# Products of six pairs made in the last attention steps, a ring of weight tiles split in two, and four sums placed ahead of the last modes

## The chip, the cores and the metric

The kernel runs on one core of one Trainium2 chip. The metric is the device time of one execution in microseconds (us). A run's profile gives a span that is about 1.8 us shorter than its device time.

A ratio is the mean time of one kernel's fast runs over the mean of the other's fast runs of the same rounds on the same chip. It is therefore not quite the ratio of the medians that are also quoted. Brackets give the 95% interval.

## The reference

```python
x = attention(q, k, v, s)                 # 8 batches, 576 rows, 8 heads of 64 -> 512 columns
X = np.fft.rfft(x, axis=1)[:, :64]        # 64 modes
Yr = Xr @ w_r - Xi @ w_i                  # per mode; w_r, w_i: 64 x 512 x 512 in float32
Yi = Xr @ w_i + Xi @ w_r
y = np.fft.irfft(Y, n=576, axis=1)
u = x + y
return u + np.maximum(u @ w_ch, 0.0)
```

The weights w_r and w_i are 134 MB in float32. They are read once and cast to bfloat16 on the way.

## The kernel before

Attention takes 32 steps: four groups of heads, each with eight batches. The modes need the four groups of columns g in turn. Each g has eight groups of modes, called modes group 0 to 7 below, and each modes group reads four weight tiles of 512 KB. So there are 128 weight tiles. The modes of the last g run after attention. Between them stands the work on w_ch: for each pair of row tiles x@w_ch is made and kept ("z"), and y@w_ch is added at the end.

The parts that the change touches are these. The ring of weight tiles and the plan of its loads:

```python
WB = 17
wpool = ctx.enter_context(tc.tile_pool(name="w_sb", bufs=WB))
...
    w = W0 + (WB + NE - W0) * (n + 1) // (B + 1) if n < B else on_chip[-1] + 4
    on_chip.append(min(w, WB + (NE if used[n] < NE else used[n])))
```

The last stage, one modes group after the other, with units of x work between them (a unit is: transpose the x of one pair, multiply by w_ch, keep the result):

```python
TAKE = (3, 3, 1, 2, 4, 3)                 # units of x work in modes groups 0 to 5
for c in range(NCK - 2):
    yb = modes(NG - 1, c)
    for x in range(TAKE[c] - 1):
        work()
    yt = y_transposed(yb)
    work()
    y_times_wch(c, yt)                    # v = y@w_ch of the group; ends with spread(), a transfer into yv
work()
...
c = NCK - 2                               # modes group 6
yb = modes(NG - 1, c)
x_transposed(0)
yt = y_transposed(yb)
x_transposed(1)
y_times_wch(c, yt)
for i in range(NPRE):
    x_times_wch(i, False)
start_u(0)
add_y(us[0], 0, 0, slice(0, GK))
yb = modes(NG - 1, NCK - 1)               # modes group 7, the last weights
...                                       # y and v of group 7, in halves
spread(NCK - 1, 1, vb)
for i in range(NPRE):
    add_y(z_of(i), i, 1, slice(0, GK))    # "the four sums": y@w_ch of pairs 0 and 1, modes groups 0 to 6
for i in range(NPRE):
    for cols in halves:
        add_last(z_of(i), i, vb, cols)    # group 7, straight from its tile
    relu(i, 2 - i)
```

`add_y` reads yv, so it waits for the spreads of the modes groups that it sums. After this the 18 pairs are finished one after the other and written out.

The softmax here doesn't subtract the row's maximum and nothing guards it: scores larger than these inputs give would overflow.

Of the kernel before, what the change touches and what calls it, by code (L numbers as in the profile page):

```python
# [9 lines left out]
FP32 = mybir.dt.float32  # L10
FP16 = mybir.dt.float16
BF16 = mybir.dt.bfloat16
ACTF = mybir.ActivationFunctionType
ALU = mybir.AluOpType
# [4 lines left out]
def kernel(  # L19
# [26 lines left out]
    MC = 8  # L46
    NCK = NM // MC
    WM = 4
    WB = 17
    LA = 3  # L50
    NF = NT - 1
    R = S // (P // 2)
# [47 lines left out]
    Ff_sb = gp.tile([P, NT, 3 * NM], FP16, name="Ff_sb")  # L100
    G_sb = gp.tile([P, SP], FP16, name="G_sb")
    wch_sb = gp.tile([P, DT, DM], FP16, name="wch_sb")
    wpool = ctx.enter_context(tc.tile_pool(name="w_sb", bufs=WB))
    spool = ctx.enter_context(tc.tile_pool(name="small_sb", bufs=2))
    auxpool = ctx.enter_context(tc.tile_pool(name="aux_psum", bufs=2, space=PSUM))

# [78 lines left out]
    NE = len(early)  # L185
    wt = {}

    def loads_w(upto):
        todo = []
        while len(wt) < min(upto, len(wq)):  # L190
            g, c, ri, par = key = wq[len(wt)]
            if len(wt) < NE:
                t = early[len(wt)]
            else:
                t = wpool.tile([P, WM, DM], BF16, name="w_sb", tag="w")
            src = (moe_w_r, moe_w_i)[ri]
            todo.append((
                t,
                src[c * MC + par : (c + 1) * MC : 2, g * P : (g + 1) * P, :].rearrange("m p e -> p m e"),
            ))  # L200
            wt[key] = t
        return todo
# [14 lines left out]
    W0 = 3  # L217
    on_chip = []
    for n in range(N):
        w = W0 + (WB + NE - W0) * (n + 1) // (B + 1) if n < B else on_chip[-1] + 4  # L220
        on_chip.append(min(w, WB + (NE if used[n] < NE else used[n])))


    nc.sync.dma_start(out=s_sb, in_=s.rearrange("b h t -> (b h) t"))
# [70 lines left out]
    def transposes(n, which):  # L295
        if n >= N:
            return
        src = loaded[n][which]
        dA, dB = ((qtA, qtB), (ktA, ktB))[which]
        g, b = divmod(n, B)  # L300
        ps = trpool.tile([P, R, RP], BF16, name="tr_ps", tag="tr")
        for r in range(R):
            for h in range(2):
                rows = slice(D * h, D * h + D)
                nc.tensor.transpose(ps[rows, r, :], src[rows, r, :], ident16[rows, rows])  # L305
        for dst, rows in ((dA, slice(0, D)), (dB, slice(D, P))):
            copy = (nc.vector.tensor_copy, nc.scalar.copy)[which == 1 and dst is dB]
            copy(  # L308
                out=dst[n % NQ][rows, :].rearrange("d (p r) -> d p r", r=R),
                in_=ps[rows].rearrange("d r p -> d p r"),  # L310
            )
# [18 lines left out]
    def scores(n, h):  # L330
        g, b = divmod(n, B)
        pidx = b * H + 2 * g + h
        qt = (qtA, qtB)[h][n % NQ]
        pt = p_sb[(2 * n + h) % NP_]
        keys = (ktA, ktB)[h][n % NQ][:, : NF * P].rearrange("c (w p r) -> c w r p", p=P, r=2)
        for r in range(2):
            ps = scpool.tile([P, 1024], FP32, name="sc_ps", tag="sc")

            for w in range(NWN):
                nc.tensor.matmul(  # L340
                    ps[:, bass.ds(w * S, W)], ident16, negm[:, bass.ts(r, W)],
                    start=True, stop=False, skip_group_check=True,
                )
            for w, i0, i1 in ((0, 0, 512), (0, 512, S), (1, W, S)):
                c0 = w * S + i0 - w * W
                nc.tensor.matmul(  # L346
                    ps[:, c0 : c0 + i1 - i0], keys[:, w, r, :], qt[:, i0:i1],
                    start=False, stop=True, skip_group_check=True,
                )
            if h == 1 and r == 0:  # L350
                scores4(n, ps[:, 2 * S - W : 2 * S - W + NL])
            for w in range(NWN):
                x = 2 * w + r
                nc.scalar.activation(  # L354
                    out=pt[:, poff[x] : poff[x] + S - w * W], in_=ps[:, w * S : (w + 1) * S - w * W],
                    func=ACTF.Exp, bias=cumt_sb[:, x, pidx : pidx + 1], scale=0.125,
                )
# [53 lines left out]
    def modes(g, c):  # L411

        ps = auxpool.tile([P, DM], FP32, name="yp", tag="aux")
        for x in range(4):
            ri, par = divmod(x, 2)
            cols = xs[g % 2].rearrange("p k r b m -> p (k r b) m")
            c0 = (48, 16)[ri] - 16 * par
            for cg in range(4):
                nc.tensor.matmul(  # L419
                    ps[32 * cg : 32 * cg + 32, :],  # L420
                    cols[:, c0 : c0 + 32, c * MC + 2 * cg + par],
                    wt[(g, c, ri, par)][:, cg, :],
                    start=(x == 0), stop=(x == 3),
                    tile_position=(0, 32 * cg), skip_group_check=True,
                )
        if g == 0:
            nc.vector.tensor_copy(out=y_acc[:, c, :], in_=ps)
        elif g < NG - 1:
            nc.vector.tensor_tensor(out=y_acc[:, c, :], in0=ps, in1=y_acc[:, c, :], op=ALU.add)
        else:  # L430
            yb = spool.tile([P, DM], FP16, name="y_sb", tag="y")
            for cols in halves if c == NCK - 1 else [slice(0, DM)]:
                nc.vector.tensor_tensor(
                    out=yb[:, cols], in0=ps[:, cols], in1=y_acc[:, c, cols], op=ALU.add
                )
            spread(c, 0, yb)
            return yb
# [5 lines left out]
        nc.sync.dma_start(out=yv[16 * c : 16 * c + 16, :, which, :], in_=rows)  # L443


    with tc.tile_pool(name="sc_psum", bufs=2, space=PSUM) as scpool, \
            tc.tile_pool(name="tr_psum", bufs=1, space=PSUM) as trpool, \
            tc.tile_pool(name="av_psum", bufs=1, space=PSUM) as avpool:
        cum_rows(0)
        transposes(0, 0)  # L450
        transposes(0, 1)
        load(loads_qkv(2))
        pad_p()
        for n in range(N):
            if n in (0, 2):
                nc.vector.memset(xs[n // 2].rearrange("p k r b m -> p (k r b m)").bitcast(FP32), 0.0)
            tails_due = loads_tails(n // B + 1)[n % B - 3 : n % B - 2] if 2 < n % B < 5 else []
            load(loads_qkv(n + LA) + tails_due, loads_w(on_chip[n]))
            cum_rows(n + 1)
            scores(n, 0)  # L460
            av(n - 1, 1)
            transposes(n + 1, 0)
            scores(n, 1)
            transposes(n + 1, 1)
            fft(n - 1)
            av(n, 0)
            for c in mode_steps.get(n, []):
                modes(c // NCK, c % NCK)
            if n == N // 2:
                nc.gpsimd.dma_start(out=wch_sb, in_=moe_w_ch.rearrange("(dt p) e -> p dt e", p=P))  # L470
        av(N - 1, 1)
        fft(N - 1)
    load(loads_w(len(wq)))
    at.close()




    pairs = [((b, T), (b, T + 1)) for b in range(B) for T in range(0, NF, 2)]
    for i, b in ((4, 0), (10, B // 2)):  # L480
        pairs.insert(i, ((b, NF), (b + 2, NF)))
    NPRE = 2
    kept = list(range(NPRE, len(pairs)))


    ways = dict(zip(kept, "esesessesesseses"))

    finpool = ctx.enter_context(tc.tile_pool(name="fin_sb", bufs=1))
    yv = finpool.tile([P, B, 2, DM], FP16, name="yv")
# [11 lines left out]
    places = [finpool.tile([P, 4 * DM], BF16, name=f"z1_{i}") for i in range(NLOC)]  # L501
    places.append(old[:, 4 * DM : 8 * DM])
    places += [y_acc[:, c : c + 2, :].rearrange("p c e -> p (c e)").bitcast(BF16) for c in (0, 2)]
    xts, z1s, zs = {}, {}, {}

    def parts(b, T):

# [24 lines left out]

    def keep(i):
        x_times_wch(i, True)
        j = kept.index(i)
        if j < len(places):
            t = places[j]
        else:
            t = wpool.tile([P, WM, DM], BF16, name="z1", tag="w").rearrange("p m e -> p (m e)")
        if ways[i] == "e":  # L540
            z1s[i] = t.bitcast(FP16).rearrange("p (y x e) -> p y x e", y=2, x=2)
            nc.scalar.copy(out=z1s[i][:, 0], in_=zs[i])
            nc.vector.tensor_tensor(
                out=z1s[i][:, 1], in0=zs[i], in1=z1s[i][:, 0], op=ALU.subtract
            )
        else:
            z1s[i] = t.bitcast(FP32).rearrange("p (x e) -> p x e", x=2)
            nc.scalar.copy(out=z1s[i], in_=zs[i])  # L548

    def y_transposed(yb):  # L550
        ps = auxpool.tile([P, DT, P], FP16, name="yt_ps", tag="aux")
# [29 lines left out]
            i = ahead.pop(0)  # L581
            keep(i)

    order_z = list(kept)
    TAKE = (3, 3, 1, 2, 4, 3)
    us, rs = {}, {}
    GK = P - 2 * MC

# [61 lines left out]
    def z_of(i):  # L650
        return [zs[i][:, x, :] for x in range(2)]

    for c in range(NCK - 2):
        yb = modes(NG - 1, c)
        for x in range(TAKE[c] - 1):
            work()
        yt = y_transposed(yb)
        work()
        y_times_wch(c, yt)
    work()  # L660
    assert not order_z and not ahead
# [9 lines left out]

    start_u(0)
    add_y(us[0], 0, 0, slice(0, GK))
    yb = modes(NG - 1, NCK - 1)

    yt = spool.tile([P, DT, P], FP16, name="yt_sb", tag="yt")
# [13 lines left out]
            )  # L690
        nc.vector.tensor_copy(out=vb[:, cols], in_=vp)
    spread(NCK - 1, 1, vb)
    for i in range(NPRE):
        add_y(z_of(i), i, 1, slice(0, GK))
    for i in range(NPRE):
        for cols in halves:
            add_last(z_of(i), i, vb, cols)
# [71 lines left out]
```

## Time and profile before

| | before |
|---|---|
| device time | 461.0 us (460.58 to 461.66, 3 runs) |
| profiled run | 462.23 us, span 460.4 us |
| PE busy | 342.2 us, 74% |
| DMA row of the slices | full to slice 36 of 40 |
| last weight tile lands (profiled run) | 421.56 us |
| work after that | 38.8 us; PE has one gap there (0.53 us), and its last matmul ends at 455.6 us |

The chain that ended last, in shares by engine (the chain line of the page), says how much rests on transfers:

```profile
DMA 70%; PE 21%; issue 3%; DVE 3%; POOL 2%; SPq 0%; DVEq 0%; POOLq 0%
```

### The profile page before, as it was taken

The page shows a single profiled execution, that of the slowest core. Times are in us where ns is not written, and L with a number is a line of the kernel's source. Part 1 is how long each engine was busy: PE and PEld are TensorE (multiplying, and loading weights), DVE is VectorE, ACT ScalarE, POOL GpSimd, SP SyncE. Part 2 cuts the span into 40 slices and gives each one's busy share as a digit, 9 for nine tenths or more (in the row PEclk, how much of TensorE's full clock was granted, in tenths as well). Part 3 has the DMA queues.
Part 4 walks back from the last instruction along what each step waited for, and adds up shares of the span by engine and source line. Part 5 has one row for each costly group of instructions (what it writes and reads, how often), then busy time and mean ns, then how long its engine had stood idle before and what let it go on. Part 6 is the DMA issues. An engine that isn't in the chain of part 4 may idle for free.

```text
span 460.4 us, 10238 instructions
## 1 busy us (share of the span) xinstructions
PE 342.2 (74%) x4153; PEld 217.0 (47%) x4185; DVE 233.2 (51%) x521; ACT 218.4 (47%) x376; POOL 183.0 (40%) x269
## 2 busy tenths in 40 slices
PE   1779888974667668876666757567959858988995
PEld 1456666653445446654444534344635424544432
DVE  6775666663334346644334443334445625562675
ACT  1585876563444427744244342444602303340895
POOL 6754555544445455434544434444422222100000
PEclk9997999998777879978778795777878979999999
DMA  9999999999999999999999999999999999994697
GB/s 173 200 203 204 201 202 203 203 204 204 204 202 203 203 201 203 204 204 203 203 202 205 205 204 204 204 204 204 204 210 210 212 215 213 211 212 89 229 309 296
DMA packets 110063, 95.16 MB, mean 207 GB/s; under 512 B 28544, under 2 KB 105216, under 8 KB 110016
## 3 DMA queue, kind: packets, MB, share of 16 engines
q0 software_dynamic: 98960, 81.81, 112.2%
q1 hardware_dynamic: 11056, 12.70, 9.1%
q8 instruction: 33, 0.54, 0.4%
q14 instruction: 14, 0.11, 0.1%
HBM read 164.66 MB, written 9.44 MB: 378 GB/s over the span
## 4 chain that ended last, share of the span: by engine, by line
DMA 70%; PE 21%; issue 3%; DVE 3%; POOL 2%; SPq 0%; DVEq 0%; POOLq 0%
DMA w_sb<-in_moe_w_i_dram 31%; DMA w_sb<-in_moe_w_r_dram 25%; DMA q<-in_q_dram 7%; PE sc_ps L346 3%; PE sc_ps L340 2%; DMA wch_sb<-in_moe_w_ch_dram 2%; DMA v<-in_v_dram 2%; PE av_ps L375 2%; PE z_ps L593 2%; PE u_ps L612 2%; PE u_ps L593 2%; PE tr_ps L305 2%; PE yp L419 1%; PE z_ps L712 1%; PE z_ps L528 1%
## 5 line engine op out<-in xcount | busy, mean ns | idle before, releaser
L354 ACT ACTIVATE p_sb<-sc_ps,cumt_sb 128x576 f16<-128x576 f32 (+1 forms) x256 | 142.2, 635 | 57.2 <-PE sc_ps L346 57.0
L208 POOL DMA_DIRECT2D w_sb<-in_moe_w_i_dram x60 | 45.1, 753 | 74.8 <-PE yp L419 19.6
L208 POOL DMA_DIRECT2D w_sb<-in_moe_w_r_dram x60 | 45.2, 754 | 69.7 <-DMA w_sb<-in_moe_w_r_dram 33.2
L208 POOL DMA_DIRECT2D v<-in_v_dram x72 | 50.8, 707 | 36.0 <-DMA v<-in_v_dram 9.3
L305 PE MATMUL tr_ps<-ident,q 64*64 64x64 bf16 x576 | 18.8, 219 | 57.5 <-DMA q<-in_q_dram 57.5
L340 PE MATMUL sc_ps<-negm,ident 128*128 128x256 bf16 x256 | 58.2, 315 | 0.2
L419 PE MATMUL yp<-w_sb,xs 128*32 128x512 bf16 x480 | 37.0, 415 | 19.6 <-DMA w_sb<-in_moe_w_i_dram 18.7
L308 DVE COPY qtA<-tr_ps 64x576 bf16<-64x576 bf16 x32 | 23.8, 743 | 52.7 <-PE tr_ps L305 52.5
L325 ACT ACTIVATE p<-sc_ps,cumt 128x64 f16<-128x64 f32 x32 | 10.1, 314 | 84.1 <-PE sc_ps L321 84.1
L308 DVE COPY ktA<-tr_ps 64x576 bf16<-64x576 bf16 x32 | 24.0, 750 | 44.6 <-PE tr_ps L305 44.6
L375 PE MATMUL av_ps<-v,p_sb 128*128 128x65 f16 x1024 | 45.4, 199 | 0.0
L305 PEld LDWEIGHTS <-q 64*64 64x64 bf16 x576 | 14.8, 130 | 60.4 <-DMA q<-in_q_dram 59.5
L375 PEld LDWEIGHTS <-p_sb 128*128 128x128 f16 x1024 | 40.4, 101 | 5.2 <-issue 1.2
L346 PE MATMUL sc_ps<-qtB,ktB 128*128 128x64 bf16 (+2 forms) x160 | 37.6, 343 | 4.2 <-issue 3.1
L346 PE MATMUL sc_ps<-qtA,ktA 65*128 65x512 bf16 (+2 forms) x192 | 37.7, 306 | 0.5 <-DMA qtA<-ncum_sb 0.5
L528 PE MATMUL z_ps<-wch_sb,xs 128*128 128x512 f16 x144 | 37.0, 405 | 0.7 <-ACT z L548 0.7
L419 PEld LDWEIGHTS <-xs 128*32 128x32 bf16 x512 | 21.7, 172 | 29.6 <-issue 26.1
L380 DVE TENSOR_REDUCE den<-av_ps 128x5 f32<-128x10 f32 x64 | 10.8, 169 | 47.0 <-PE av_ps L375 46.9
L385 DVE TENSOR_TENSOR x_all<-av_ps,rcp 128x320 f16<-128x320 f32 x64 | 31.5, 492 | 2.2
L346 PEld LDWEIGHTS <-ktB 128*128 128x128 bf16 x192 | 23.9, 125 | 17.2 <-issue 8.8
L308 ACT COPY ktB<-tr_ps 64x576 bf16<-64x576 bf16 x32 | 20.3, 634 | 21.6 <-DVE ktA L308 21.1
L305 PE MATMUL tr_ps<-ident,k 64*64 64x64 bf16 x576 | 17.9, 213 | 15.0 <-DVE qtB L308 8.4
(96 smaller groups left out, 498.5 us busy)
## 6 DMA issues: line engine op xcount, KB each, us to landing
w_sb<-in_moe_w_r_dram POOLq DMA_DIRECT2D x60, 512.0 KB, 11.9
w_sb<-in_moe_w_i_dram POOLq DMA_DIRECT2D x60, 512.0 KB, 11.9
q<-in_q_dram POOLq DMA_DIRECT2D x32, 144.0 KB, 9.9
k<-in_k_dram POOLq DMA_DIRECT2D x32, 144.0 KB, 10.3
v<-in_v_dram POOLq DMA_DIRECT2D x72, 64.0 KB, 10.0
out_dram<-r_sb SPq DMA_DIRECT2D x16, 256.0 KB, 2.5
out_dram<-r_w SPq DMA_DIRECT2D x16, 256.0 KB, 2.6
x_all<-in_moe_w_i_dram POOLq DMA_DIRECT2D x3, 512.0 KB, 9.9
```

Of the source, the lines that this page charges most:

```text
L208: nc.gpsimd.dma_start(out=dst, in_=src)
L305: nc.tensor.transpose(ps[rows, r, :], src[rows, r, :], ident16[rows, rows])
L308: copy(out=dst[n % NQ][rows, :].rearrange("d (p r) -> d p r", r=R), in_=ps[rows].rearrange("d r p -> d p r"),)
L340: nc.tensor.matmul(ps[:, bass.ds(w * S, W)], ident16, negm[:, bass.ts(r, W)], start=True, stop=False, skip_group_check=True,)
L346: nc.tensor.matmul(ps[:, c0 : c0 + i1 - i0], keys[:, w, r, :], qt[:, i0:i1], start=False, stop=True, skip_group_check=True,)
L354: nc.scalar.activation(out=pt[:, poff[x] : poff[x] + S - w * W], in_=ps[:, w * S : (w + 1) * S - w * W], func=ACTF.Exp, bias=cumt_sb[:, x, ...
L375: nc.tensor.matmul(ps[:, I, r : r + NCH], lhsT, rhs, start=(i == 0), stop=(i == len(todo) - 1), skip_group_check=True,)
L380: nc.vector.tensor_reduce(out=den, in_=ps[:, :, 0 : VW : NCH], axis=mybir.AxisListType.X, op=ALU.add)
L385: nc.vector.tensor_tensor(out=x_all[:, g, b, :, D * h : D * h + D], in0=ps[:, :, 1 : NCH], in1=rcp.unsqueeze(2).to_broadcast([P, NT, D]), ...
L419: nc.tensor.matmul(ps[32 * cg : 32 * cg + 32, :], cols[:, c0 : c0 + 32, c * MC + 2 * cg + par], wt[(g, c, ri, par)][:, cg, :], start=(x == ...
L528: nc.tensor.matmul(z[:, x, :], xts[i][:, x, dt, :], wch_sb[:, dt, :], start=(dt == 0), stop=(last and dt == DT - 1), skip_group_check=True,)
L593: nc.tensor.matmul(dst[x][r, :], G_sb[rows, bass.ds(T * P, r.stop - r.start)], yv[rows, bb, which, :], start=start, stop=True, skip_group_ ...
```

## The change

The intent: use PE's idle time in the last attention steps for the x@w_ch of six pairs, so that the last stage has less to do, and take four matmuls out of the stretch behind the last weight. To keep six products from attention on, the ring of 17 weight tiles becomes two, of 11 and 6. The 6 hold weights up to tile 75 and then the products.

```diff
-    WB = 17
+    WA, WB = 11, 6
-    wpool = ctx.enter_context(tc.tile_pool(name="w_sb", bufs=WB))
+    wpool = ctx.enter_context(tc.tile_pool(name="w_sb", bufs=WA))
+    wpool2 = ctx.enter_context(tc.tile_pool(name="w2_sb", bufs=WB))
...
+    LW2 = 76
+    def ring_of(k):
+        if k < NE:
+            return None
+        return int(k < LW2 and (k - NE) % (WA + WB) >= WA)
...                                  # on_chip: + 5 for + 4, and a count of free slots by ring
+            if i is not None:
+                first_transposed(i, 0)
             transposes(n + 1, 1)
             fft(n - 1)
             av(n, 0)
+            if i is not None:
+                first_product(i, 0)
+                first_transposed(i, 1)
             for c in mode_steps.get(n, []):
                 modes(c // NCK, c % NCK)
+            if i is not None:
+                first_product(i, 1)
...
-    TAKE = (3, 3, 1, 2, 4, 3)
+    TAKE = (2, 2, 1, 2, 0, 3)
...
     start_u(0)
     add_y(us[0], 0, 0, slice(0, GK))
+    for i in range(NPRE):
+        add_y(z_of(i), i, 1, slice(0, GK))
     yb = modes(NG - 1, NCK - 1)
...
     spread(NCK - 1, 1, vb)
-    for i in range(NPRE):
-        add_y(z_of(i), i, 1, slice(0, GK))
```

More of the change, by code (lines that the diff above doesn't have):

```diff
@@ L191, in loads_w @@
             g, c, ri, par = key = wq[len(wt)]
-            if len(wt) < NE:
+            i = ring_of(len(wt))
+            if i is None:
                 t = early[len(wt)]
             else:
-                t = wpool.tile([P, WM, DM], BF16, name="w_sb", tag="w")
+                t = (wpool, wpool2)[i].tile([P, WM, DM], BF16, name="w_sb", tag="w")
             src = (moe_w_r, moe_w_i)[ri]
@@ L219 @@
     for n in range(N):
-        w = W0 + (WB + NE - W0) * (n + 1) // (B + 1) if n < B else on_chip[-1] + 4
-        on_chip.append(min(w, WB + (NE if used[n] < NE else used[n])))
+        w = W0 + (WA + WB + NE - W0) * (n + 1) // (B + 1) if n < B else on_chip[-1] + 5
+        nt, ring = 0, ([], [])
+        while nt < min(w, len(wq)):
+            i = ring_of(nt)
+            if i is not None:
+                depth = (WA, WB)[i]
+                if len(ring[i]) >= depth and ring[i][-depth] >= used[n]:
+                    break
+                ring[i].append(nt)
+            nt += 1
+        on_chip.append(nt)
     nc.sync.dma_start(out=s_sb, in_=s.rearrange("b h t -> (b h) t"))
@@ L443, in spread, with kept_place, keep_product, first_transposed @@
         nc.sync.dma_start(out=yv[16 * c : 16 * c + 16, :, which, :], in_=rows)
+    pairs = [((b, T), (b, T + 1)) for b in range(B) for T in range(0, NF, 2)]
+    for i, b in ((4, 0), (10, B // 2)):
+        pairs.insert(i, ((b, NF), (b + 2, NF)))
+    NPRE = 2
+    kept = list(range(NPRE, len(pairs)))
+    ways = dict(zip(kept, "esesessesesseses"))
+    first_pairs = [i for i in kept if pairs[i][0][1] < NF and pairs[i][0][0] <= 3]
+    z1s, xts1 = {}, {}
+    def kept_place(i, t):
+        if ways[i] == "e":
+            z1s[i] = t.bitcast(FP16).rearrange("p (y x e) -> p y x e", y=2, x=2)
+        else:
+            z1s[i] = t.bitcast(FP32).rearrange("p (x e) -> p x e", x=2)
+    def keep_product(i, xx, z):
+        if ways[i] != "e":
+            nc.scalar.copy(out=z1s[i][:, xx], in_=z)
+            return
+        nc.scalar.copy(out=z1s[i][:, 0, xx], in_=z)
+        nc.vector.tensor_tensor(out=z1s[i][:, 1, xx], in0=z, in1=z1s[i][:, 0, xx], op=ALU.subtract)
+    def first_transposed(i, x):
+        b, T = pairs[i][x]
+        ps = auxpool.tile([P, DT, P], FP32, name="xt_ps", tag="aux")
+        for dt in range(DT):
+            nc.tensor.matmul(
+                ps[:, dt, :], x_all[:, dt, b, T, :], ident16h, start=True, stop=True,
+                skip_group_check=True,
+            )
+        xts1[i, x] = spool.tile([P, DT, P], FP16, name="xt1", tag="yt")
+        nc.vector.tensor_copy(out=xts1[i, x], in_=ps)
+    def first_product(i, x):
+        if x == 0:
+            t = wpool2.tile([P, WM, DM], BF16, name="z1", tag="w").rearrange("p m e -> p (m e)")
+            kept_place(i, t)
+        ps = auxpool.tile([P, DM], FP32, name="z1_ps", tag="aux")
+        for dt in range(DT):
+            nc.tensor.matmul(
+                ps, xts1[i, x][:, dt, :], wch_sb[:, dt, :], start=(dt == 0), stop=(dt == DT - 1)
+            )
+        keep_product(i, x, ps)
     with tc.tile_pool(name="sc_psum", bufs=2, space=PSUM) as scpool, \
@@ L463 @@
             scores(n, 1)
+            i = first_pairs[n - N + len(first_pairs)] if n >= N - len(first_pairs) else None
+            if i is not None:
+                first_transposed(i, 0)
             transposes(n + 1, 1)
@@ L466 @@
             av(n, 0)
+            if i is not None:
+                first_product(i, 0)
+                first_transposed(i, 1)
             for c in mode_steps.get(n, []):
                 modes(c // NCK, c % NCK)
+            if i is not None:
+                first_product(i, 1)
             if n == N // 2:
@@ L474 @@
     at.close()
-    pairs = [((b, T), (b, T + 1)) for b in range(B) for T in range(0, NF, 2)]
-    for i, b in ((4, 0), (10, B // 2)):
-        pairs.insert(i, ((b, NF), (b + 2, NF)))
-    NPRE = 2
-    kept = list(range(NPRE, len(pairs)))
-    ways = dict(zip(kept, "esesessesesseses"))
     finpool = ctx.enter_context(tc.tile_pool(name="fin_sb", bufs=1))
@@ L503 @@
     places += [y_acc[:, c : c + 2, :].rearrange("p c e -> p (c e)").bitcast(BF16) for c in (0, 2)]
-    xts, z1s, zs = {}, {}, {}
+    xts, zs = {}, {}
     def parts(b, T):
@@ L534, in keep @@
         x_times_wch(i, True)
-        j = kept.index(i)
+        j = late.index(i)
         if j < len(places):
@@ L539, in keep @@
             t = wpool.tile([P, WM, DM], BF16, name="z1", tag="w").rearrange("p m e -> p (m e)")
-        if ways[i] == "e":
-            z1s[i] = t.bitcast(FP16).rearrange("p (y x e) -> p y x e", y=2, x=2)
-            nc.scalar.copy(out=z1s[i][:, 0], in_=zs[i])
-            nc.vector.tensor_tensor(
-                out=z1s[i][:, 1], in0=zs[i], in1=z1s[i][:, 0], op=ALU.subtract
-            )
-        else:
-            z1s[i] = t.bitcast(FP32).rearrange("p (x e) -> p x e", x=2)
-            nc.scalar.copy(out=z1s[i], in_=zs[i])
+        kept_place(i, t)
+        keep_product(i, slice(0, 2), zs[i])
     def y_transposed(yb):
@@ L582, in work @@
             keep(i)
-    order_z = list(kept)
-    TAKE = (3, 3, 1, 2, 4, 3)
+    late = [i for i in kept if i not in first_pairs]
+    order_z = list(late)
+    TAKE = (2, 2, 1, 2, 0, 3)
     us, rs = {}, {}
@@ L657 @@
         yt = y_transposed(yb)
-        work()
+        if TAKE[c]:
+            work()
         y_times_wch(c, yt)
```

## The prediction

> **What bounds the kernel now.** I read the page's forty slices first, because they show which limit rules which stretch.
>
> ```profile
> PE   1779888974667668876666757567959858988995
> DMA  9999999999999999999999999999999999994697
> GB/s 173 200 203 204 201 202 203 203 204 204 204 202 203 203 201 203 204 204 203 203 202 205 205 204 204 204 204 204 204 210 210 212 215 213 211 212 89 229 309 296
> ```
>
> The DMA row is full from the first slice to slice 36 (414 us) at a flat 200 to 215 GB/s, while PE is loose. Only in the last three and a half slices does that turn round. The windows view cuts the same at the arrival of the last weight tile (columns: PE, PEld, DVE, ACT, POOL busy, granted clock, DMA share, GB/s):
>
> ```profile
> 0.00:340.00 340.00, 243.65 (x3501) 168.58 (x3534) 168.82 (x424) 170.80 (x322) 166.62 (x247) 0.85 1.28 202
> 340.00:421.60 81.60, 65.19 (x480) 33.82 (x480) 39.81 (x57) 19.84 (x23) 16.33 (x22) 0.90 1.19 204
> 430.00:440.00 10.00, 10.00 (x51) 4.02 (x50) 7.07 (x12) 8.82 (x9) 0.00 (x0) 1.00 0.78 264
> ```
>
> So there are two stages in series: **transfers to 421.6 us**, then **38.8 us of PE work** (460.4 - 421.6) in which PE has no gap. The chain that ended last says the same:
>
> ```profile
> 376.83 21.11 DMA w_sb<-in_moe_w_i_dram
> ...
> 398.48 23.09 DMA w_sb<-in_moe_w_i_dram
> 421.56 0.04 issue
> 421.61 0.48 PE yp L419 x3
> ```
>
> A weight tile lands 21 to 23 us after its issue, and the next issue of the chain stands at the landing of the one eight tiles before. The order of the GpSimd queue shows why: each transfer waits for the landing of the eighth before it, so eight are in flight. Tiles land about 2.5 us apart: the queue in front of the DMA engines is about 20 us deep, and PE could be late by much of that before the engines ran dry. What PE waited for between 405 and 430 us on weights is small:
>
> ```profile
> PE yp L419 <- DMA w_sb<-in_moe_w_i_dram: 1.3, 1, 1.3
> ```
>
> [...] the 128 KB spreads of y and v, issued from SyncE, take 6.0 us (median) while weights stream and 2.9 us once they have ended. [...] The page of this kernel counts 378 GB/s read and written over the span, with casting loads that write 2 bytes for 4 read; so I take the 204 to 213 GB/s written as full rate, not as idleness that deeper prefetch could fill. [...] 0.76 granted in 220 to 300 us, 1.00 from 380 us on. [...] In this trace PE runs its program in order, so a wait put ahead of the last modes holds those up too.
>
> **Part 1: six pairs of x@w_ch made earlier.** In the stage from 340 us the 16 kept pairs and the 2 of the end cost PE z_ps at L528 x144, 8 a pair; back to back, 8 take 1.73 us and the 8 transposes 0.45 us at full clock. Six pairs therefore move 6 x 2.2 = 13 us of PE, 6 x 2 x 0.68 = 8.2 us of DVE copies and some 6 us of ACT copies from the last stage into steps 26 to 31. That is 2.2 us of PE a step. A step that waited for no transfer took 6.2 us (330 to 336 us, no transposes) to about 7.4 with transposes and modes; a step paced by DMA takes 12.5. With 2.2, plus about 1 us of waiting for the two PSUM buffers, a step becomes 10 to 11 us, still under 12.5. **Worth on the path: 0**, at both ends: the end of transfers rests on bytes, and no byte is removed. The copies split into halves cost ACT 2 x 0.59 for 1.02 us, beside other work.
>
> **Part 2: the ring of 17 split into 11 and 6.** Up to tile 75 the split turns over in the order of one ring of 17; from tile 76 on, weights have only the 11. Working out the two load schedules from the code gives, after steps 25, 28 and 31, 85, 97, 109 tiles asked for before and 86, 91, 103 after. Six tiles fewer ahead of the last q, k and v bring these some 6 x 2.5 = 15 us earlier at most; the same tiles then follow. What matters is whether 11 slots starve the engines. Step 29's tiles 91 to 94 need slots freed by the modes of step 28, and so on, four a step. From landings (tile 80 at 284.9 us, 2.5 us a tile, 2.4 us for a step's q, k, v) I get tiles 94, 98, 102 landed at about 330, 340, 350 us; at 10.5 us a step from k of step 29 at 304, PE frees the next four at about 319, 330, 340. Each is 10 us ahead of need. In the last stage a modes group frees 4 as it ends, with 7 others in flight, 17 us of transfer. So **0**, with a margin of four tiles. The later part of the ring is equal too: result tiles reuse the slots of tiles 120 to 127 in either kernel.
>
> **Part 3: four sums ahead of the last modes.** This alone touches the path. Before, in the timeline of the end:
>
> ```profile
> 410.80 1.12 PE L419 MATMUL yp<-w_sb,xs 128*32 128x512 bf16 x16
> ...
> 415.92 0.55 SPq L443 DMA_DIRECT2D yv<-v_sb  x1
> ...
> 418.88 0.60 PE L593 MATMUL u_ps<-yv,G_sb 112*128 112x512 f16 x2
> 419.41 0.90 PE L419 MATMUL yp<-w_sb,xs 128*32 128x512 bf16 x12
> 421.61 0.45 PE L419 MATMUL yp<-w_sb,xs 128*32 128x512 bf16 x4 [1.29 <-DMA w_sb<-in_moe_w_i_dram]
> ...
> 424.35 1.03 PE L593 MATMUL z_ps<-yv,G_sb 112*128 112x512 f16 x4
> ```
>
> *Saved:* the four L593 matmuls after the modes, 0.87 us in the chain. But they filled the time in which DVE copied v_sb (424.11 to 424.97): without them the L602 matmuls wait for the second half until about 425.0 and end near 425.7 in place of 426.25. Saved 0.55 us.
>
> *Paid:* they read v of the sixth modes group (counted from 0), whose spread was issued at 415.92 and took 5.5 us: 421.4. With no work taken in group 4, PE reaches group 5 at the landing of its last tile (398.0, not 399.2), and group 6 at its own (410.0, not 410.8), so the last matmuls of group 6 end 1.3 us earlier; the spread is issued near 414.6 and lands at 420.2 (421.0 if the others slow it). PE stands in front of it. Then 0.87 us of sums, then 16 modes matmuls of 1.1 us: 422.2 in place of 422.06, up to 423.0. The last weight has landed by then, so PE, no longer the weight, sets this point. Paid 0.15 to 0.95 us.
>
> **Sum:** 0 + 0 - 0.55 + (0.15 to 0.95) = -0.4 to +0.4. With a little for the looser PE in the last stage: 461.0 - 0.2 = **460.8 us**.
>
> **Rivals.** (a) *The ring of 11 starves the DMA* around 330 to 355 us. For it: four tiles a step are freed only as fast as PE steps, and the steps grow. Against it: the 10 us of margin. If steps took 14 us, the three from 29 to 31 would eat it and the end would slip 1 to 5 us: 462 to 466. (b) *The wait for v becomes the bound*: a spread in 7 us instead of 5.5 (the slowest took 7.5), and perhaps PE idle long enough to fall to half clock: 462 to 463, or 464 with the clock. Against it: PE idles 2.3 us there at most by my count, and 1.3 us did no harm before. (c) *PE was the hidden bound of the last stage*, so that 13 us less of it pulls the end in: 455 or less. For it: PE is 8 to 9 tenths busy there. Against it: the DMA is full throughout; modes groups 0 to 4 and 7 end at the landing of their own tiles, and the groups late by about 1 us cost nothing at the end.
>
> **Range and chances.** Runs before spread 1.1 us; the two sides of part 3 give 0.4 each way; (a) and (b) lengthen the upper side. 459.8 to 462.2. Two per cent is 9.2 us: only (c) gives that downward, and only an (a) far beyond my count upward. Faster 0.02, same 0.96, slower 0.02.
>
> **What would show it.** Right: the last weight tile lands at 421 to 422 us; DMA row full to slice 36; granted clock higher in 300 to 350 us; PE waiting 1 to 3 us on the v spread (L654) just ahead of the last modes, and no wait for weights in those; the tail after them shorter by 0.5 us. Wrong: gaps in the DMA row or GB/s under 200 between 320 and 360 us (a); a wait over 3 us on the spread (b); the last tile landing well before 420 us (c).

Cuts in this text are marked. They told of the hardware what no trace of this case shows. No term of the sum is cut: it came to 0 + 0 - 0.55 + (0.15 to 0.95), that is -0.4 to +0.4, and to 460.8 us with the 0.2 taken off. These figures belong beside what is left:

- The 14 spreads that were issued before the last weight landed took 5.5 to 7.5 us, the two behind it 2.94 and 2.87 (the trace of before).
- The 0.76 and 1.00 are the granted clock (windows view). PE was busy for 53.8 of the 80 us at 0.76, and for 35.8 of the 41.6 us from 380 us to 421.6. The clock records hold two values only, 1.00 and 0.50.
- That 204 to 213 GB/s is the full rate was the author's estimate. It rests on the 378 GB/s of the profile page and on a DMA row that is full at 200 to 215 GB/s. No run tried for more.
- Of the 257 GpSimd transfers of before from the ninth on, none was issued until the eighth before it had landed; the nearest stands 0.28 us behind that landing. So no more than eight were in flight. The queue 20 us deep is an estimate from this (eight times 2.5 us), and that PE could be late by much of it was not shown.
- PE in order: in the changed kernel the modes of group 7 start at 421.47 us, behind the four sums (420.52), though their last weight had landed at 420.11.
- The 1 us of waiting for two PSUM buffers is an estimate; the longest such wait in the last stage of before is 0.66 us (390.86).
- Rival (b): that 2.3 us of idle time would leave the clock full was an estimate that no trace showed. In filler26, below, half clock followed on 1.59 us.

## The result, and the profile after

| | before | after |
|---|---|---|
| device time, same rounds | 461.46 us (460.58 to 462.08, 6 runs) | 462.46 us (462.16 to 463.4, 6 runs) |
| ratio | | 1.0027 [1.0012, 1.0042] |
| span of the profiled run | 460.4 us | 460.6 us |

The changed kernel is slower by 0.27%, about 1.2 us. That is "the same" at 2%, as predicted. But 0.2 us faster was predicted, and 462.46 lies above the range given, 459.8 to 462.2. The two profiled spans differ by only 0.2 us, because the profiled run of before was slower than its timed runs.

The slices of the changed kernel's page (PE busy, granted clock, DMA busy, GB/s):

```profile
PE   1779877966663969947397676888977766589995
PEclk9997999997777979968778979799987789599999
DMA  9999999999999999999999999999999999993697
GB/s 175 201 203 203 202 201 203 203 204 204 204 204 200 203 199 203 204 205 204 202 200 205 204 204 204 204 202 203 206 210 214 214 214 214 214 210 81 228 309 297
```

The DMA row is as full as before, also in slices 28 to 31 (322 to 368 us), where the ring of 11 might have starved it. The new thing is the 5 in the clock row at slice 34. The windows view shows that stretch, 398.4 to 403 us, just behind modes group 5 (columns as in the prediction). First before, then after:

```profile
387.00:398.40 11.40, 9.94 (x73) 5.53 (x73) 6.79 (x10) 3.53 (x4) 2.98 (x4) 1.00 1.23 214
398.40:403.00 4.60, 4.60 (x46) 2.61 (x44) 2.58 (x4) 1.37 (x2) 0.74 (x1) 1.00 1.24 206
```

```profile
387.00:398.40 11.40, 4.67 (x28) 1.35 (x27) 1.39 (x2) 0.58 (x1) 2.97 (x4) 0.60 1.22 217
398.40:403.00 4.60, 4.60 (x20) 2.15 (x20) 1.89 (x3) 0.00 (x0) 0.74 (x1) 0.51 1.24 206
```

With TAKE 0 in modes group 4, PE is busy for 4.67 us of 11.4 in place of 9.94. The clock stands at half from 389.2 to 402.9 us, and the work behind group 5 starts at 0.51: its first eight z matmuls take 3.43 us (from 399.78) in place of the 1.89 of the kernel before. The timeline of the end (columns as in the prediction) shows what follows:

```profile
411.40 1.12 PE L438 MATMUL yp<-w_sb,xs 128*32 128x512 bf16 x16
...
416.51 0.55 SPq L462 DMA_DIRECT2D yv<-v_sb  x1
...
419.57 0.60 PE L654 MATMUL u_ps<-yv,G_sb 112*128 112x512 f16 x2
420.52 1.02 PE L654 MATMUL z_ps<-yv,G_sb 112*128 112x512 f16 x4 [0.34 <-issue]
421.47 1.12 PE L438 MATMUL yp<-w_sb,xs 128*32 128x512 bf16 x16
422.65 0.76 DVE L452 TENSOR_TENSOR y_sb<-yp,y_acc 128x256 f16<-128x256 f32 x2 [6.17 <-PE yp L438]
```

Group 6 starts at 411.40. Its last tile had landed at 408.92 (the DMA view: issued 387.40, 21.5 us to landing). Then come the four sums (L654 into z_ps), and only at 421.47 the modes of group 7, without any wait for weights: the last tile had landed at 420.11. The chain that ended last tells the same, for it no longer goes through the last weight:

```profile
398.36 0.67 PE yp L438 x3
...
415.75 3.45 PE z_ps L595 x16
...
420.52 1.02 PE z_ps L654 x4
421.54 1.09 PE yp L438 x12
422.65 0.44 DVE y_sb L452
```

From 398 us on this chain is work of PE with a few copies, and the sums are a piece of it. **PE has become the bound of the last 20 us of the transfer stage.**

### The profile page after: what moved, and what is told of

The parts are those of the page before. It is cut to its first block, busy times and chain, and to the rows that moved or that the text cites. A ratio compares the mean times of both kernels' runs of the same rounds, so it can differ in the third digit from the quotient of the medians.

```text
span 460.6 us, 10231 instructions
## 1 busy us (share of the span) xinstructions
PE 342.9 (74%) x4153; PEld 216.4 (47%) x4185; DVE 233.5 (51%) x523; ACT 219.2 (48%) x382; POOL 182.8 (40%) x269
## 4 chain that ended last, share of the span: by engine, by line
DMA 66%; PE 20%; DVE 6%; issue 4%; POOL 2%; SPq 0%; DVEq 0%; POOLq 0%
DMA w_sb<-in_moe_w_i_dram 29%; DMA w_sb<-in_moe_w_r_dram 20%; DMA q<-in_q_dram 15%; PE z_ps L595 3%; PE sc_ps L365 2%; PE z_ps L654 2%; PE tr_ps L324 2%; PE yp L438 2%; PE u_ps L673 2%; PE u_ps L654 2%; PE sc_ps L359 2%; PE z_ps L774 1%; PE av_ps L394 1%; POOL w_sb L217 1%; DMA xs<-c_negm 1%
## 5 line engine op out<-in xcount | busy, mean ns | idle before, releaser
L438 PE MATMUL yp<-w_sb,xs 128*32 128x512 bf16 x480 | 38.1, 414 | 26.1 <-DMA w_sb<-in_moe_w_i_dram 21.2
L359 PE MATMUL sc_ps<-negm,ident 128*128 128x256 bf16 x256 | 56.3, 306 | 0.2
L324 PE MATMUL tr_ps<-ident,q 64*64 64x64 bf16 x576 | 17.7, 212 | 51.7 <-DMA q<-in_q_dram 51.7
L324 PEld LDWEIGHTS <-q 64*64 64x64 bf16 x576 | 13.8, 124 | 54.4 <-DMA q<-in_q_dram 53.3
L365 PE MATMUL sc_ps<-qtB,ktB 128*128 128x64 bf16 (+2 forms) x160 | 35.2, 326 | 3.7 <-issue 2.4
L365 PEld LDWEIGHTS <-ktB 128*128 128x128 bf16 x192 | 22.7, 118 | 15.2 <-issue 6.6
L595 PE MATMUL z_ps<-wch_sb,xs 128*128 128x512 f16 x96 | 28.4, 452 | 0.0
```

The source lines that it names most:

```text
L324: nc.tensor.transpose(ps[rows, r, :], src[rows, r, :], ident16[rows, rows])
L359: nc.tensor.matmul(ps[:, bass.ds(w * S, W)], ident16, negm[:, bass.ts(r, W)], start=True, stop=False, skip_group_check=True,)
L365: nc.tensor.matmul(ps[:, c0 : c0 + i1 - i0], keys[:, w, r, :], qt[:, i0:i1], start=False, stop=True, skip_group_check=True,)
L438: nc.tensor.matmul(ps[32 * cg : 32 * cg + 32, :], cols[:, c0 : c0 + 32, c * MC + 2 * cg + par], wt[(g, c, ri, par)][:, cg, :], start=(x == ...
L595: nc.tensor.matmul(z[:, x, :], xts[i][:, x, dt, :], wch_sb[:, dt, :], start=(dt == 0), stop=(last and dt == DT - 1), skip_group_check=True,)
```

## The experiments

The theories when the experiments began. **T1**: PE has become late at the end, by the sums and by the cold clock (half of full speed granted, 0.51 in 398.4 to 403 us) behind group 5. **T2**: the ring of 11 or the added attention work slows the transfers. **T3**: the sums alone are the loss. Ten runs were made: eight edited kernels, and each of the two kernels once more. All were correct. The table puts the profiles side by side. "y_sb" is the start of the DVE addition behind modes group 7, the point at which the kernel is done with its weights.

| kernel | last weight lands | y_sb starts | y_sb behind last weight | y_sb to end | ratio to before |
|---|---|---|---|---|---|
| before, first profile | 421.56 | 422.11 | 0.55 | 38.3 | |
| before_again | 420.50 | 421.05 | 0.55 | 38.1 | 0.9995 [0.9974, 1.0015] |
| after | 420.11 | 422.65 | 2.54 | 38.0 | 1.0027 [1.0012, 1.0042] |
| after_again | 420.45 | 423.00 | 2.55 | 38.0 | 1.0028 [1.0002, 1.0055] |
| sums_back | 419.88 | 421.08 | 1.20 | 38.1 | 1.0005 [0.9989, 1.0021] |
| before_sums_ahead | 420.98 | 423.70 | 2.72 | 38.1 | 1.0028 [1.0011, 1.0045] |
| take_shift | 420.68 | 423.53 | 2.85 | 39.4 | 1.0039 [1.0019, 1.0058] |
| take_shift_sums_back | 420.70 | 421.25 | 0.55 | 40.2 | 1.0008 [0.9990, 1.0025] |
| filler | 421.15 | 423.68 | 2.53 | 37.7 | 1.0020 [1.0002, 1.0038] |
| filler26 | 420.46 | 424.00 | 3.54 | 39.0 | 1.0037 [1.0008, 1.0065] |
| early_warm | 420.99 | 421.54 | 0.55 | 38.0 | 0.9992 [0.9976, 1.0007] |
| direct6 | 421.09 | 421.83 | 0.74 | 37.8 | 1.0006 [0.9986, 1.0025] |

Two columns do the work. "y_sb behind last weight" is 0.55 where PE stood ready. It grows to 2.5 and more where the sums stand ahead and wait for the spread of v. "y_sb to end" is about 38, and more where the clock fell. The last weight lands anywhere from 419.88 to 421.56 us without a pattern by kernel, so one profile's landing is good to about a microsecond only. Each profile is also of one run out of six, and not always of a middling one: those of take_shift, take_shift_sums_back and filler26 are of the slowest run of the six.

### sums_back: part 3 undone, parts 1 and 2 kept

```diff
     add_y(us[0], 0, 0, slice(0, GK))
-    for i in range(NPRE):
-        add_y(z_of(i), i, 1, slice(0, GK))
     yb = modes(NG - 1, NCK - 1)
...
     spread(NCK - 1, 1, vb)
+    for i in range(NPRE):
+        add_y(z_of(i), i, 1, slice(0, GK))
```

> The changed kernel with part 3 undone: the four y@w_ch sums of pairs 0 and 1 stand behind the last modes again. Theory T1 (PE has become late at the end: in the profile of after the last weight had landed at 420.11 us, yet the last modes group began at 421.47, behind the sums): without the sums the last modes start at about 420.2, y_sb near 421.3 in place of 422.65, and the tail grows by 0.55 again, so 0.5 to 0.9 us faster than after (about 461.7 when after is 462.4), still 0.3 to 0.7 us slower than before because group 6 is still late. Rival T2 (the ring of 11 slots or the added attention work slows the transfers): no change from after, ratio to before 1.002 to 1.003. Rival T3 (the sums are the whole loss): equal to before, ratio 1.000 or under.

461.61 us (median of 6) beside 461.16 for before, ratio 1.0005: equal to before. This is what T3 expected. It speaks against T2, as the ring and the early pairs are all in this kernel, though the interval just reaches T2's 1.002; early_warm below, which has them too, ends at 1.0007. T1's figure (0.3 to 0.7 us over before) lies inside the interval too. The timeline of its end:

```profile
411.29 1.12 PE L438 MATMUL yp<-w_sb,xs 128*32 128x512 bf16 x16
...
419.91 1.12 PE L438 MATMUL yp<-w_sb,xs 128*32 128x512 bf16 x16
```

Group 6 is as late as in the changed kernel. Without the sums PE still comes to group 7 at 419.91, as the last weight lands (419.88). So the lateness of group 6 is just covered, and nothing is left to cover the sums.

### before_sums_ahead: part 3 alone, in the kernel before

```diff
     add_y(us[0], 0, 0, slice(0, GK))
+    for i in range(NPRE):
+        add_y(z_of(i), i, 1, slice(0, GK))
     yb = modes(NG - 1, NCK - 1)
...
-    for i in range(NPRE):
-        add_y(z_of(i), i, 1, slice(0, GK))
```

> The kernel before with part 3 alone: the four sums moved ahead of the last modes, ring and load plan untouched. If the sums ahead are the loss whatever the rest (theory now: they put 0.87 us of matmuls and the wait for the v spread between PE and modes whose weights have landed, and give back only 0.4 us behind them): ratio to before 1.001 to 1.004, and in the profile the last modes start after the spread of v has landed plus 0.87 us. If the sums hurt only together with the early pairs and the smaller ring: ratio 0.998 to 1.000.

462.97 us beside 462.09, ratio 1.0028: the whole loss of the change, made by part 3 alone. The end of its timeline:

```profile
421.57 1.02 PE L593 MATMUL z_ps<-yv,G_sb 112*128 112x512 f16 x4 [0.82 <-issue]
422.53 1.12 PE L419 MATMUL yp<-w_sb,xs 128*32 128x512 bf16 x16
```

The sums start as the spread of v lands (421.49), after a wait of 0.82 us, and hold PE 0.96 us more. The last weight had landed at 420.98. In this one profile all of PE's work from group 5 on came about 1.3 us later than in the first of before (group 6 at 412.07), though nothing ahead of the sums was edited; so the ratio of six runs, and not the 2.72 us of the table, is what measures the cost.

### before_again: the kernel before against itself

```diff
(no edit)
```

> The kernel before against itself: ratio 1.000 within the interval, which shows what the method resolves. Its profile is a second look at when the last weight lands (421.56 us in the first profile, whose run of 462.2 us was slower than all three timed ones): if the last weight lands near 420.3 to 420.8 here, the 1.29 us that PE waited before the last modes in the first profile was partly a slow run's, and the room on which the prediction counted was smaller.

Ratio 0.9995 [0.9974, 1.0015]: the method finds no difference where there is none, and a difference of 0.2% is about what it can resolve. The second profile is more telling:

```profile
420.55 0.45 PE L419 MATMUL yp<-w_sb,xs 128*32 128x512 bf16 x4 [0.23 <-DMA w_sb<-in_moe_w_i_dram]
```

PE waits 0.23 us for the last weight, not the 1.29 us of the first profile. All of PE's own times are the same (group 6 starts at 410.79 and 410.80, group 7 at 419.40 and 419.41). Only the landing moved, by 1.06 us. So the idle time in which the prediction let the sums hide varies from run to run, from 0.23 to 1.29 us in two profiles. The second run, 460.94 us, was on the fast side (the medians of before are 461.08 to 462.09 us), so a middling run lies between the two.

### after_again: the changed kernel once more

```diff
(no edit)
```

> The changed kernel once more, for a second profile and six more times beside the same runs of the kernel before. If the sums ahead of the last modes are the loss: ratio to before 1.002 to 1.004 again, and in the profile the last modes start 1.0 to 1.6 us after the last weight has landed, behind the four sums. If the first measurement was a chance of its chip: 0.999 to 1.001.

462.7 us beside 461.08, ratio 1.0028 on another set of rounds. In the second profile y_sb stands 2.55 us behind the last weight; it was 2.54 in the first. The last modes start 1.37 us after that landing (421.82), as expected.

### take_shift: one unit of work moved from group 5 to group 4

```diff
-    TAKE = (2, 2, 1, 2, 0, 3)
+    TAKE = (2, 2, 1, 2, 1, 2)
```

> The changed kernel with one unit of work moved from modes group 5 to group 4: TAKE (2, 2, 1, 2, 1, 2) for (2, 2, 1, 2, 0, 3); sums still ahead. T1: PE has less to do at half clock after group 5, so group 6 starts at the landing of its last tile (near 409 us) and not at 411.4; the sums then wait for the v spread (landing 419.5 to 420.5) and the last modes begin near 420.7 in place of 421.5: 0.5 to 1.0 us faster than after, about equal to before (ratio 0.999 to 1.001). T2: as after, 1.002 to 1.003. T3 (sums alone): as after.

462.93 us, ratio 1.0039: **a miss for T1**, which expected an equal of before. Group 6 did start on time, its last four matmuls at 409.28, as the last tile landed at 409.23. But being early did not help:

```profile
420.34 1.25 PE L654 MATMUL z_ps<-yv,G_sb 112*128 112x512 f16 x4 [1.86 <-issue]
421.52 1.97 PE L438 MATMUL yp<-w_sb,xs 128*32 128x512 bf16 x16
```

PE stands 1.86 us in front of the spread of v, which lands at 420.25. Then the clock falls to half, from 421.0 to 427.8 us by its records, and the 16 modes matmuls take 1.97 us in place of 1.12. This profile is of the slowest of the six runs (464.71 us; the others 462.01 to 463.77), so how many of them went cold is not known.

### take_shift_sums_back: both edits

```diff
-    TAKE = (2, 2, 1, 2, 0, 3)
+    TAKE = (2, 2, 1, 2, 1, 2)
(and the edit of sums_back)
```

> Both edits: TAKE (2, 2, 1, 2, 1, 2) and the sums behind the last modes. T1: PE is early at group 6 and group 7, the last modes wait for their last weight again, so the end is that of the transfers plus the tail of before: 1.0 to 1.5 us faster than after, ratio to before 0.998 to 1.000. T2: still 1.002 to 1.003, as the ring and the six early pairs are all in it. T3: ratio 1.000, the same as with the sums back alone.

461.42 us, ratio 1.0008. It is 1.4 us faster than take_shift in the same rounds, again what the sums cost, but not under before, as T1 had expected. The timeline of its profiled run shows one cost:

```profile
420.75 0.45 PE L438 MATMUL yp<-w_sb,xs 128*32 128x512 bf16 x4 [2.44 <-DMA w_sb<-in_moe_w_i_dram]
...
424.28 1.91 PE L654 MATMUL z_ps<-yv,G_sb 112*128 112x512 f16 x4
```

PE is now 2.44 us early. It waits for the last weight as it should, and behind the wait the clock stands at half, from 422.7 to 426.1 us. The same four sums take 1.91 us behind the modes, 1.03 in the kernel before, and y_sb to the end is 40.2 us in place of 38.1. But this is the slowest run of the six (463.24 us; the other five 461.05 to 461.92), so it does not explain their median; whether they went cold is not known. What the profile does show is that y_sb is 0.55 us behind the last weight, as in before: where the weight sets this point, PE gains nothing by coming earlier.

### early_warm: ten matmuls that nobody reads, in that wait

```diff
     add_y(us[0], 0, 0, slice(0, GK))
+    warm = auxpool.tile([P, DM], FP32, name="warm_ps", tag="aux")
+    for k in range(10):
+        nc.tensor.matmul(warm, yt[:, k % DT, :], wch_sb[:, k % DT, :], start=True, stop=True,
+                         skip_group_check=True)
     yb = modes(NG - 1, NCK - 1)
(on top of take_shift_sums_back)
```

> take_shift_sums_back with 10 matmuls of 128x512 that nobody reads put ahead of the last modes, in the 2.44 us in which PE stood idle there. In take_shift_sums_back the clock stood at half from 422.7 to 426.1 us and the v_ps and z_ps matmuls took 1.71 us each in place of 0.87. If the idle wait is what cools the clock: full clock from 420 to 430 us, the tail from the last landing to the end 38.3 to 38.8 us in place of 40.7, and the time 0.5 to 1.5 us below take_shift_sums_back (ratio to before 0.997 to 1.000; the timed runs of take_shift_sums_back may have been cold only in part). If the clock does not matter: the same as take_shift_sums_back, 1.0008.

461.6 us beside 462.09, ratio 0.9992 [0.9976, 1.0007]: where expected, though its interval and that of take_shift_sums_back overlap, so no gain is shown by the times. The profile:

```profile
417.42 2.32 PE L738 MATMUL warm_ps<-wch_sb,yt_sb 128*128 128x512 f16 x10
...
423.77 1.03 PE L654 MATMUL z_ps<-yv,G_sb 112*128 112x512 f16 x4
```

Full clock through the end (1.00 in 411 to 455 us), the four sums back to 1.03 us, and y_sb to the end 38.0 us in place of 40.2. It fits that the idle wait was what cooled the clock, and so do the twelve profiles together: the three in which PE stood idle for 1.59, 1.86 and 2.44 us just ahead of or within the last modes had half clock behind it, and the nine with 1.29 us or less there did not. The half clock began 0.6 us (filler26), 0.7 us (take_shift) and about 2 us (take_shift_sums_back) after work had begun again. But the length of one gap does not settle it: in before PE stood idle for 1.62 us ahead of the matmuls at 387.03, and the clock stayed at 1.00 from 380.6 to 459.2 us, while the 1.59 us of filler26 were followed by half clock.

### filler and filler26: matmuls that nobody reads ("idle matmuls"), behind group 4

```diff
         y_times_wch(c, yt)
+        if c == 4:
+            warm = auxpool.tile([P, DM], FP32, name="warm_ps", tag="aux")
+            for k in range(18):            # 26 in filler26
+                nc.tensor.matmul(warm, yt[:, k % DT, :], wch_sb[:, k % DT, :], start=True, stop=True,
+                                 skip_group_check=True)
(on top of the changed kernel)
```

> The changed kernel with 18 matmuls of 128x512 into a PSUM tile that nobody reads, between modes groups 4 and 5, where PE stood idle; nothing moved. It keeps the TensorE clock from standing at half (0.51 granted in 398.4 to 403.0 us of after). If the cold clock is the cause of the late group 6: granted clock near 1.0 in 398 to 403 us, group 6 starts at 409 to 409.8 us and not at 411.4, and the time falls 0.4 to 0.9 us below after. If the lateness comes from the amount of work after group 5 alone, group 6 still starts at about 411 us and the time stays as after. T2: as after.

The 18 were too few. That they would keep the clock from half was a guess that this run denies: they ended at 396.4 us, the last tile of group 5 landed at about 399.2, and the clock fell again (half from 399.7 to 403.1 us). Group 6 started at 411.85, still 2 us behind its last tile. This run does not decide the question; its time, 462.56 us and ratio 1.0020, is that of the changed kernel within the intervals.

> The changed kernel with 26 idle matmuls between modes groups 4 and 5 in place of the 18 of the first attempt, which ended 2.9 us before the last tile of group 5, so that the clock fell again (0.50 granted from 399.7 to 403.1 us). If the half clock is what makes group 6 late in the changed kernel: full clock from 398 to 411 us, 10.5 us of work behind group 5 as in the kernel before, in place of 12.5 to 13.0, so group 6 starts within 0.8 us of the landing of its last tile; the sums then wait longer for the v spread, so the time falls by 0.5 us at most, ratio to before 1.001 to 1.003. If the lateness is the amount of work alone: group 6 starts 2 us or more after its last tile, as in after (408.92 and 411.40).

With 26 the clock is full from 394 to 421 us, and the question is decided:

```profile
409.56 1.12 PE L438 MATMUL yp<-w_sb,xs 128*32 128x512 bf16 x16
...
420.72 1.33 PE L654 MATMUL z_ps<-yv,G_sb 112*128 112x512 f16 x4 [1.59 <-issue]
421.98 1.96 PE L438 MATMUL yp<-w_sb,xs 128*32 128x512 bf16 x16
```

From the end of group 5 (399.03) to group 6 it takes 10.5 us, as in the kernel before, in place of 12.5. **The half clock is what made group 6 late in the changed kernel.** It starts 1.24 us behind its last tile rather than the 0.8 expected, since the idle matmuls themselves held group 5 up a little. The time did not fall: 463.59 us, ratio 1.0037, above the 1.001 to 1.003 expected. PE, early again, stands 1.59 us in front of the spread and goes cold at 421.3 us. The six times fall in two clumps, 461.66, 461.81 and 462.75 on one side and 464.43, 464.68 and 464.81 on the other. The profiled run, with the cold end, is the 464.81. That the other clump kept its clock is likely, but no profile of it was taken.

### direct6: sums that do not wait for the spread

```diff
-        add_y(z_of(i), i, 1, slice(0, GK))
+        add_y(z_of(i), i, 1, slice(0, GK - 2 * MC))       # groups 0 to 5 only
+        add_last(z_of(i), i, v6, gx=Gx6_sb)               # group 6 straight from its v_sb tile
(on top of take_shift; Gx6_sb is made like Gx_sb, with the rows of group 6; add_last takes it as gx)
```

> take_shift with the sums still ahead, but over groups 0 to 5 alone (their spreads landed by 413 us), and group 6 added to z straight from its v_sb tile with a second constant, as the last group is; four matmuls more, no wait for the v spread of group 6. If the wait for that spread and the cold clock behind it are what take_shift lost: no wait above 0.5 us ahead of the sums, last modes at the landing of their last weight, full clock in the tail, and 1.5 to 2.5 us below take_shift (ratio to before 0.996 to 1.000, better than both kernels if under 0.999). If the sums are lossy for another reason (the tail behind them gains nothing): 1.001 to 1.003.

462.05 us beside 462.09, ratio 1.0006 [0.9986, 1.0025]. The timeline of its end:

```profile
418.82 0.60 PE L659 MATMUL z_ps<-yv,G_sb 96*128 96x512 f16 x2
...
420.12 0.59 PE L668 MATMUL z_ps<-v_sb,Gx_sb 128*128 128x512 f16 x2
420.65 1.12 PE L441 MATMUL yp<-w_sb,xs 128*32 128x512 bf16 x16
```

No wait, full clock from 420 us on (1.00 to 455 us, after 0.81 in 411 to 420), and the modes start at 420.65, before the last weight lands (421.09). With the sums still ahead, the loss of take_shift is gone within the interval. It is not better than before: it lies between the two expectations (to 1.000 if wait and clock were the whole loss, from 1.001 if the sums lose for another reason), and its interval reaches into both. No version was found that beats both kernels by more than the method resolves.

## Why the prediction was wrong

**The bound: right.** The last weight lands at 419.9 to 421.6 us in every profile, and 37.7 to 40.2 us follow from y_sb to the end. Two readings were loose: PE is not without a gap there, and the last 24 tiles landed 2.8 us apart in the mean, not 2.5, with the spreads among them. Nothing hangs on either.

**Part 1, six pairs earlier, worth 0: right.** sums_back holds parts 1 and 2 and is equal to before (1.0005). The steps behave as worked out: in the changed kernel the small exponentials of steps 27 to 31 start at 290.1, 301.6, 311.2, 321.8 and 331.4 us, so steps of 9.6 to 11.5 us against the 10 to 11 predicted. The sign given for it came too: the granted clock in 300 to 350 us rose from 0.77 to 0.93, with PE busy for 43.4 of these 50 us in place of 36.2. Rival (c), that PE was the hidden bound of the whole last stage, falls with it, as less of PE in that stage moved nothing. But the stage did not lose the 13 us of PE that were counted at full clock. From 340 to 420 us, before and after:

```profile
340.00:420.00 80.00, 64.87 (x480) 33.76 (x480) 39.81 (x57) 19.84 (x23) 16.33 (x22) 0.90 1.21 208
340.00:420.00 80.00, 57.74 (x380) 28.29 (x380) 30.49 (x45) 13.95 (x17) 16.30 (x22) 0.81 1.19 209
```

PE's busy time fell by 7 us, since the granted clock fell from 0.90 to 0.81 with it: not quite half of the 13 us came back as slower work.

**Part 2, the ring, worth 0: right.** The DMA row is full and GB/s does not fall under 202 from slice 26 to slice 35, where the weights end. Rival (a) did not happen.

**Part 3: wrong, and this is the failed step**: "Paid 0.15 to 0.95 us" against "Saved 0.55 us". The path was right: PE, and no longer the weight, sets the point from which the end runs. Three terms were off.

1. *The time at which the last weight lands.* The step set 422.2 to 423.0 against the 422.06 of the first profile, in which PE had 1.29 us to spare. In the second profile it had 0.23. Most of the spare time was that of one run, and the list of timed runs (461.0 us beside 462.23 for the profiled one) could have told so. This term makes the difference: against the first profile y_sb moved by 0.54 us only (422.11 to 422.65), as foretold, and against the second by 1.60.
2. *PE's arrival at group 6.* "With no work taken in group 4, PE reaches ... group 6 at its own (410.0)". The work was counted at full clock. In the idle time that TAKE 0 makes the clock stayed at half until 402.9, and group 6 started at 411.40. That is 0.6 us later than before (410.79), not 0.8 us earlier. filler26 shows the cause: with a full clock it is 409.56. The prediction had thought of half clock, but only for the wait ahead of the last modes (rival (b)). It was luck that the last modes still ended where foretold (422.59, foretold 422.2 to 423.0): the spread was issued at 416.51, not 414.6, but took 3.92 us in place of 5.5, as it outlasted the last weight (two spreads wholly behind that weight took 3.50 and 2.91), and so landed at 420.43, foretold 420.2 to 421.0.
3. *The saving.* From y_sb to the second pair's first u_ps matmul it is 3.98 us before (422.11 to 426.09) and 3.57 after (422.65 to 426.22), so 0.41 saved of the 0.55 predicted. At the end of the kernel 0.1 to 0.4 us of it are left (38.1 and 38.3 against 38.0 twice).

The sum with the measured terms: y_sb started at 421.05 us in the second profile of before and at 422.65 after, so 1.60 paid where at most 0.95 was foretold. Of this 0.61 is the late group 6, 0.95 the sums (420.52 to 421.47) and 0.34 the wait for v; less the 0.23 us that PE had waited for the weight before, that makes 1.67, which is 0.07 too much and not accounted for. With 0.1 to 0.4 saved, 1.2 to 1.5 us remain, and 1.2 us were timed.

sums_back shows that the 0.61 alone would have cost little: without the sums PE arrives just as the last weight lands. before_sums_ahead shows that the sums alone cost the whole. So T3 is right about what costs, T1 about how (PE late at the last weights), and T2 falls.

**Rival (b), the wait for v and a cold clock: right as a mechanism, but not in this kernel.** After the change the wait was 0.34 and 0.56 us in the two profiles, because PE came late; the 1 to 3 us of waiting and the tail shorter by 0.5 us, which the prediction gave as signs of its being right, did not show. In take_shift and filler26, where PE comes early, the wait is 1.86 and 1.59 us and the clock falls, as rival (b) had it.

## What to carry to other kernels

An instruction moved ahead of a wait is free only if the engine has that much idle time in a typical run (here 0.95 us of sums met 1.29 us of it in one profile and 0.23 in the other): take the idle time from two profiles, or from a profile whose time agrees with the timed ones. PE ran its program in order here, so what is moved ahead of the last arrival must not itself wait for a transfer that lands at about the same time (in before_sums_ahead PE stood 0.82 us in front of the spread, which landed 0.5 us behind the last weight). And PE that comes early is no gain by itself: in the three profiles in which it stood idle for 1.6 to 2.4 us ahead of the last stage, part of that stage ran at half clock, and y_sb to the end took 39.0 to 40.2 us in place of 38.1.
